# A memory-attention and mixture-of-experts kernel on one core: the half tile's outputs copied before their low parts, W2's split moved to GpSimd in the first layer, W1 loaded in four transfers

## The chip, the cores and the metric

The kernel runs on 1 core of one Trainium2 chip. The metric is the device time of one execution in microseconds (us). Before the change the median of 3 runs is 473.84 us (473.26 to 475.56).

## What is computed

Attention over 32 memory slots in each of 8 batches and 8 heads, and then a layer of 8 experts (one per token) over the 4608 tokens of width 512:

```
a     = softmax(phi)                       # over 32 slots, per token and head
k_m   = einsum('bhsm,bhsd->bhmd', a, k);   v_m = einsum('bhsm,bhsd->bhmd', a, v)
x     = softmax(q @ k_m.T / 8) @ v_m       # heads side by side: (4608, 512)
e     = argmax(normalized(x) @ normalized(expert_emb).T / tau)   # and its softmax weight
out   = weight * (relu(x @ w1[e]) @ w2[e]) # w1: 512 x 1024, w2: 1024 x 512
```

## The kernel before

**One expert per batch.** Work goes batch by batch (b = 0 to 7, 576 tokens each). The kernel counts which expert most tokens of a batch chose (`choose`, L146), loads that expert's W1 and W2, and runs all tokens of the batch through it. Tokens with another expert are done after the last batch by a loop (`rest`) that runs only where there are any.

**Low parts.** A matmul in full fp32 takes several passes. The large products are therefore made of three passes over rounded operands: high by high, high by low, low by high. A tensor's high part is a copy to fp32r, its low part the difference. So attention weights have `aT` (high and low), the projected W1 `gh` and `gl`, the hidden layer `hh` and `hl`, and W2 `wh` and `wl`.

**A batch has three stages on TensorE.**
- `project` (L531) multiplies the batch's values with W1: four PSUM tiles `pg`. ScalarE rounds each to gh, VectorE subtracts for gl.
- `first` (L546) makes the hidden layer: 16 groups of six matmuls, eight (f = 0 to 7) for each half of the tokens (s = 0, 1), each into a PSUM tile `ph` of 128 x 288. ScalarE applies Relu into hh (L560), VectorE makes hl from the same PSUM tile and hh (L561), and in the second half ScalarE copies the last 64 tokens in plain fp32 as `h4`, called h in the trace (L565).
- `second` (L568) makes the output in five tiles. The first is the half tile: the last 64 tokens, 32 plain fp32 matmuls of h4 by w2s (L579). Then four tiles of 128 tokens follow, each of 8 groups of three matmuls (L590). ScalarE scales each result by the tokens' weight into `ys`, and GpSimd issues the store.

The PSUM tiles pg, ph, py and some of po share four buffers (`mm`), so a group of the first layer can begin only when the tile four before it has been read.

**W2's split.** `split_w` (L524) rounds one of W2's eight row blocks into wh (with `scalar.copy` unless another copy is given) and has GpSimd subtract for wl (L528). `must` in `batch` (L670) makes sure that a block is split, in the order of the program, before the first tile uses it.

**The order is written by hand.** Every engine works through its own queue in the program's order. `steps` (L607) makes two lists of places: `first[0..15]`, one after each group of the first layer, and `second[0..39]`, one after each group of the second (0 to 7 the half tile, 8 to 15 the first tile, and so on). While batch b goes through its layers, these places hold the attention of batch b+1 and the softmax of batch b+2:
- `fill`, `weigh` and `divide` are VectorE's work on the scores of b+1, one half g at a time: transpose (L63), maximum (L70), subtract it (L72), ScalarE's Exp (L74), then sum (L81), a small add (L82), reciprocal (L83), product (L84), and `turn` transposes the result into `aw` (L90, L92).
- `attend` (L94) multiplies aw with the values on TensorE (`po`, L101), and `norm` follows on VectorE.
- `choose` counts the experts, and SyncE loads W1 (`load_w1`, L358) and W2 (`load_w2`, L364), `parts` splits aw (GpSimd subtracts, L518), and `keep` stores aw and the values to DRAM.
- `late` (L211) is the row of small VectorE operations on 128 x 5 and 128 x 40 elements that make the tokens' weights (L179 to L208), with one Exp on ScalarE (L198) in between. Batch 0 does its own in `first`, between the groups; the other batches have theirs in the second layer of the batch before.

SyncE's DMAs take eight semaphores in turn, and each waits for the one issued eight before it.

Of the kernel before, what the change touches and what calls it, by code (L numbers as in the profile page):

```python
# [12 lines left out]
AF = mybir.ActivationFunctionType  # L13
# [8 lines left out]
N, DM, E, FF = B * S, H * D, 8, 1024  # L22
NG = 2
NC = 4
# [4 lines left out]
HS = S // 2  # L29
# [187 lines left out]
class Kernel:  # L217
# [139 lines left out]

    def load_w1(self, e, halves=False):  # L358

        for k in range(2):  # L360
            c, f = (slice(NC), slice(512 * k, 512 * k + 512)) if halves else (slice(2 * k, 2 * k + 2), slice(FF))
            self.nc.sync.dma_start(self.w1s[:, c, f], self.w1[bass.ds(e, 1), :, c, f].rearrange("a p c f -> (a p) c f"))

    def load_w2(self, e):  # L364
# [181 lines left out]
    def first(self, n):  # L546

        nc = self.nc
        gh, gl, (ah, al) = self.gh, self.gl, self.aT
        for s in range(2):  # L550
            to = slice(s * HS, s * HS + HS)
            for f in range(8):
                p = self.mm([P, HS], f"ph{n}_{s}{f}")
                fs = slice(f * P, f * P + P)
                for g in range(NG):
                    for k, (w, x) in enumerate(((gh, ah), (gh, al), (gl, ah))):
                        nc.tensor.matmul(  # L557
                            p, lhsT=w[:, g, fs], rhs=x[:, g, to], start=g == 0 and k == 0, stop=g == 1 and k == 2
                        )
                nc.scalar.activation(self.hh[:, f, to], p, AF.Relu)  # L560
                nc.vector.scalar_tensor_tensor(  # L561
                    out=self.hl[:, f, to], in0=p, scalar=0.0, in1=self.hh[:, f, to].bitcast(F32), op0=ALU.max, op1=ALU.subtract
                )
                if s:
                    nc.scalar.activation(self.h4[:, f], p[:, HS - 64 :], AF.Relu)  # L565
                yield

    def second(self, n, gate, put, must):  # L568
# [38 lines left out]
    def steps(self, b, t, u):  # L607


        first, second = ([[] for _ in range(n)] for n in (16, 40))  # L610

        for f in (0, 3, 6) if b else ():
            first[f].append(lambda: self.split_w(self.nc.gpsimd.tensor_copy))
        for f in () if b else (9, 11, 13, 15):
            first[f].append(self.split_w)
        for n in (0, 1, 2, 4, 5) if b else (0, 0, 1, 1):
            second[n].append(self.split_w)
        if not b:
            late = t.late()
            first[1] += [lambda: self.flip(1, 0), lambda: t.attend(4)]  # L620
# [5 lines left out]
        if u:  # L626
            c, o = b + 1, 0 if b else 3
            first[0 + o].append(lambda: self.block(c, 1))
            first[2 + o].append(lambda: self.flip(c, 1))
            first[4 + o].append(lambda: self.scores(c))  # L630

            places = (first[6], first[8], first[10], first[12]), (first[12], first[14], second[0], second[3])
            if not b:
                places = (second[0], second[0], second[0], second[4]), (second[4], second[4], second[4], second[7])
            all = slice(0, BL)
            for g in range(NG):
                work = u.weigh((g,), all)
                places[g][0].append(lambda g=g: u.fill((g,), all, [self.sT[:, i] for i in range(NG)]))
                for at in places[g][1:]:
                    at.append(lambda work=work: next(work, None))  # L640
            for at, g in zip((second[0], second[3]) if b else (second[4], second[7]), range(NG)):
                at.append(lambda g=g: (u.divide((g,), all), u.turn((g,), all)))
            o = 0 if b else 7
            second[14 + o].append(lambda: u.attend(0, 1, pt=self.mm))
            second[15 + o].append(lambda: u.norm(0, 1))
            second[16 + o].append(lambda: u.attend(2, 3))
            second[17 + o].append(lambda: u.norm(2, 3))
            second[18 + o].append(lambda: u.attend(4, pt=self.mm))
            second[20 + o] += [lambda: self.load_w2(u.choose()), lambda: u.norm(4), self.parts, lambda: self.keep(c)]
            second[21 + o] += [u.owner, u.flags]  # L650
            after = u.late()
            for n in (24, 25, 26, 28, 29, 30):
                second[n + o].append(lambda: next(after))
            second[30 + o].append(lambda: list(after))
            m = b + 2
            if m < B:
                for g in range(NG):
                    second[11 + 3 * g + o].append(lambda g=g: self.softmax(m, (g,)))
                second[18 + o].append(lambda: self.shares(m))
                second[22 + o].append(lambda: [self.turn(m, i, min(i + 4, 10)) for i in (0, 4, 8)])  # L660
                second[27 + o] += [lambda: self.slots(m, 0), lambda: self.block(m, 0)]
                second[31 + o].append(lambda: self.flip(m, 0))
        return first, second

    def batch(self, b, t, u):
# [248 lines left out]
```

## Time and profile before

| | |
|---|---|
| median of 3 runs | 473.84 us |
| the profiled execution | 472.12 us, of which the span is 470.2 us |
| TensorE's mean granted clock | 0.979 |
| busy TensorE (PE), its weight loads (PEld) | 428.2 us, 337.7 us |
| busy VectorE (DVE), ScalarE (ACT), GpSimd (POOL) | 287.0 us, 196.5 us, 145.1 us |
| HBM read, written | 66.60 MB, 15.20 MB |
| W1: DMAs of 1024 KB, median to landing | 16, 6.4 us |
| W2: DMAs of 512 KB, median to landing | 32, 10.1 us |

A timeline row gives start, duration (us), engine, line, operation, output<-input, shape and count, and in brackets how long the engine sat idle before it and what ended that. A group row ends with busy us, mean ns of one, and the idle time before them with its releaser. Matmuls overlap, so from start to start they are closer than their durations. In a row of stretches stand the busy time of PE, PEld, DVE, ACT and POOL, then the granted clock (1.00 is full), the DMA share and GB/s. SPq and POOLq are queues that issue DMAs.

### The profile page before, as it was taken

Reading aid. Unit: us, or ns where it says so; the run is one execution under the profiler, and the core shown is the slowest. Engines: PE = TensorE matmul, PEld = TensorE weight load, DVE = VectorE, ACT = ScalarE, POOL = GpSimd, SP = SyncE. Lnnn points to the kernel's source line nnn. Section 1 sums busy time; section 2 is a strip of 40 time slices with the busy share of each in tenths; the row PEclk is TensorE's granted clock in tenths of the full one; section 3 lists DMA queues with packets and bytes.
Section 4 is the critical chain, followed back from the end, with each engine's and each line's share of the span. In section 5 each row is a group of like instructions: output and inputs, shape, how many; then the busy total and the mean of one; then the engine's idle time right before and its main releaser. Section 6 shows DMA issues by size and latency. Waiting matters only on the chain. (4 is left out here: it accounts for less than half of the span.)

```text
span 470.2 us, 9244 instructions
## 1 busy us (share of the span) xinstructions
PE 428.2 (91%) x3516; PEld 337.7 (72%) x3516; DVE 287.0 (61%) x838; ACT 196.5 (42%) x510; POOL 145.1 (31%) x153
## 2 busy tenths in 40 slices
PE   3779989999799998999799997999979998999994
PEld 2548748777687967879487775878768795869683
DVE  5685687658873687536972587636787368646100
ACT  4524553366423553345341663235633354225410
POOL 1020281251523242350630515313332506224500
PEclk9869999999999999999999998999999999999998
DMA  8977801894069801985029910498017600292011
GB/s 303 350 279 237 312 0 58 294 333 191 13 224 337 301 1 33 329 305 208 12 92 379 328 67 12 169 365 314 15 36 278 209 1 1 55 369 98 13 46 48
DMA packets 27584, 82.45 MB, mean 175 GB/s; under 512 B 7080, under 2 KB 7464, under 8 KB 25744
## 3 DMA queue, kind: packets, MB, share of 16 engines
q1 hardware_dynamic: 24736, 73.28, 43.8%
q0 software_dynamic: 2688, 8.26, 4.9%
q8 instruction: 29, 0.48, 0.4%
q10 hardware_dynamic: 112, 0.28, 0.2%
q14 instruction: 19, 0.16, 0.1%
HBM read 66.60 MB, written 15.20 MB: 174 GB/s over the span
## 5 line engine op out<-in xcount | busy, mean ns | idle before, releaser
L528 POOL TENSOR_TENSOR wl<-w2s,wh 128x512 fp32r<-128x512 f32 x64 | 85.3, 1353 | 128.5 <-ACT wh L527 126.8
L590 PE MATMUL py<-wl,hh 128*128 128x512 f32 x256 | 102.6, 401 | 6.0 <-POOL wl L528 5.7
L557 PE MATMUL ph<-aT,gh 128*128 128x288 f32 x512 | 105.3, 300 | 1.0 <-DVE gl L541 0.5
L590 PE MATMUL py<-wh,hh 128*128 128x512 f32 x256 | 105.7, 413 | 0.0
L590 PE MATMUL py<-wh,hl 128*128 128x512 f32 x256 | 100.6, 393 | 0.0
L561 DVE SCALAR_TENSOR_TENSOR hl<-ph,hh 128x288 fp32r<-128x288 f32 x128 | 56.7, 455 | 49.0 <-ACT hh L560 48.8
L557 PEld LDWEIGHTS ph<-aT,gh 128*128 128x128 f32 x512 | 81.4, 188 | 5.8 <-DVE gl L541 2.6
L557 PE MATMUL ph<-aT,gl 128*128 128x288 f32 x256 | 75.3, 294 | 0.0
L590 PEld LDWEIGHTS py<-wl,hh 128*128 128x128 f32 x256 | 48.5, 189 | 21.5 <-POOL wl L528 13.2
L560 ACT ACTIVATE hh<-ph 128x288 fp32r<-128x288 f32 x128 | 51.0, 411 | 21.6 <-PE ph L557 21.6
L590 PEld LDWEIGHTS py<-wh,hh 128*128 128x128 f32 x256 | 48.4, 189 | 12.7 <-issue 3.9
L590 PEld LDWEIGHTS py<-wh,hl 128*128 128x128 f32 x256 | 48.4, 189 | 10.1
L698 POOL DMA_DIRECT2D out_dram<-ys x28 | 15.5, 553 | 110.7 <-ACT ys L603 71.3
L541 DVE TENSOR_TENSOR gl<-pg,gh 128x512 fp32r<-128x512 f32 x32 | 20.0, 685 | 48.0 <-ACT gh L540 48.0
L557 PEld LDWEIGHTS ph<-aT,gl 128*128 128x128 f32 x256 | 48.0, 188 | 0.0
L603 ACT ACTIVATE ys<-py,gate 128x512 f32<-128x512 f32 (+1 forms) x39 | 25.0, 641 | 55.1 <-issue 29.4
L518 POOL TENSOR_TENSOR aT<-aw,aT 128x576 fp32r<-128x576 f32 (+2 forms) x18 | 23.3, 1310 | 61.3 <-DVE aT L517 61.3
L101 PE MATMUL po<-vv,aw 128*128 128x136 f32 x160 | 26.0, 298 | 11.7 <-DVE aw L90 11.7
L101 PEld LDWEIGHTS po<-vv,aw 128*128 128x128 f32 x160 | 23.7, 201 | 16.0 <-DVE aw L90 13.4
L579 PE MATMUL py<-w2s,h 128*64 128x256 f32 x256 | 31.3, 386 | 4.0 <-ACT h L565 4.0
L565 ACT ACTIVATE h<-ph 128x64 f32<-128x64 f32 x64 | 14.3, 224 | 34.3 <-DVE hl L561 34.3
L579 PEld LDWEIGHTS py<-w2s,h 128*64 128x64 f32 x256 | 16.3, 136 | 16.6 <-ACT h L565 10.7
(140 smaller groups left out, 545.0 us busy)
## 6 DMA issues: line engine op xcount, KB each, us to landing
kx<-kv SPq DMA_DIRECT2D x32, 512.0 KB, 6.6
w1s<-w SPq DMA_DIRECT2D x16, 1024.0 KB, 6.4
w2s<-w SPq DMA_DIRECT2D x32, 512.0 KB, 10.1
qt<-qT SPq DMA_DIRECT2D x14, 576.0 KB, 6.5
out_dram<-ys POOLq DMA_DIRECT2D x28, 256.0 KB, 5.8
ex<-phiT SPq DMA_DIRECT2D x16, 288.0 KB, 10.8
ad<-aw SPq DMA_DIRECT2D x8, 576.0 KB, 13.7
kl<-kvt SPq DMA_DIRECT2D x7, 256.0 KB, 3.7
```

Source lines behind the costliest of these rows:

```text
L101: nc.tensor.matmul(po[:, 144 * g : 144 * g + P + E], lhsT=k.aw[:, g, to], rhs=k.vv[:, g], start=True, stop=True)
L518: self.nc.gpsimd.tensor_tensor(out=al, in0=a, in1=ah.bitcast(F32), op=ALU.subtract)
L528: self.nc.gpsimd.tensor_tensor(out=l, in0=x, in1=h.bitcast(F32), op=ALU.subtract)
L541: nc.vector.tensor_tensor(out=self.gl[:, g, f], in0=ps[g], in1=self.gh[:, g, f].bitcast(F32), op=ALU.subtract)
L557: nc.tensor.matmul(p, lhsT=w[:, g, fs], rhs=x[:, g, to], start=g == 0 and k == 0, stop=g == 1 and k == 2)
L560: nc.scalar.activation(self.hh[:, f, to], p, AF.Relu)
L561: nc.vector.scalar_tensor_tensor(out=self.hl[:, f, to], in0=p, scalar=0.0, in1=self.hh[:, f, to].bitcast(F32), op0=ALU.max, op1=ALU.subtract)
L565: nc.scalar.activation(self.h4[:, f], p[:, HS - 64 :], AF.Relu)
L579: nc.tensor.matmul(p[64 * j : 64 * j + 64], lhsT=self.h4[:, f], rhs=self.w2s[:, f, d * j : d * j + d], start=f == 0, stop=f == 7,)
L590: nc.tensor.matmul(p, lhsT=h[:, f, to], rhs=w[:, f], start=f == 0 and k == 0, stop=f == 7 and k == 2)
L603: nc.scalar.activation(y[:, :d], p, AF.Copy, scale=gate[:, i : i + 1])
L698: eng.dma_start(self.out[r : r + P], y)
```

## The change

There are four edits.
- W1 comes in four DMAs of 512 KB where it came in two of 1 MB: for batch 0 by halves of the columns and pairs of row blocks, else by row block.
- In the second half of the first layer, h4's Relu on ScalarE now stands directly behind hh's, ahead of VectorE's hl.
- W2's split: in batches 1 to 7, all eight blocks are rounded and subtracted on GpSimd at `first[0]` to `first[7]`, where three were and five were rounded on ScalarE in the second layer. In batch 0 two blocks each stand at `first[8]`, `[10]`, `[12]` and `[14]`, one rounded on ScalarE and one on GpSimd; they were all rounded on ScalarE, four at `first[9]` to `[15]` and four in the second layer.
- The attends, `choose` with the loads of W1 and W2, `parts`, `keep`, `owner`, `flags` and the turn of the next softmax stand one place later in the second layer; the first attend so comes behind the first tile's last group and no longer ahead of it.

```
     def load_w1(self, e, halves=False):
-        for k in range(2):
-            c, f = (slice(NC), slice(512 * k, 512 * k + 512)) if halves else (slice(2 * k, 2 * k + 2), slice(FF))
+        for k in range(4):
+            i, j = divmod(k, 2)
+            c, f = (slice(2 * j, 2 * j + 2), slice(512 * i, 512 * i + 512)) if halves else (slice(k, k + 1), slice(FF))
...
                 nc.scalar.activation(self.hh[:, f, to], p, AF.Relu)
+                if s:
+                    nc.scalar.activation(self.h4[:, f], p[:, HS - 64 :], AF.Relu)
                 nc.vector.scalar_tensor_tensor(
                     out=self.hl[:, f, to], in0=p, scalar=0.0, in1=self.hh[:, f, to].bitcast(F32), op0=ALU.max, op1=ALU.subtract
                 )
-                if s:
-                    nc.scalar.activation(self.h4[:, f], p[:, HS - 64 :], AF.Relu)
...
-        for f in (0, 3, 6) if b else ():
-            first[f].append(lambda: self.split_w(self.nc.gpsimd.tensor_copy))
-        for f in () if b else (9, 11, 13, 15):
-            first[f].append(self.split_w)
-        for n in (0, 1, 2, 4, 5) if b else (0, 0, 1, 1):
-            second[n].append(self.split_w)
+        for j in range(8):
+            copy = self.nc.gpsimd.tensor_copy if b or j % 2 else None
+            first[j if b else 8 + j // 2 * 2].append(lambda copy=copy: self.split_w(copy))
...
-            second[14 + o].append(lambda: u.attend(0, 1, pt=self.mm))
+            second[15 + o].append(lambda: u.attend(0, 1, pt=self.mm))
...
-            second[20 + o] += [lambda: self.load_w2(u.choose()), lambda: u.norm(4), self.parts, lambda: self.keep(c)]
-            second[21 + o] += [u.owner, u.flags]
+            second[21 + o] += [lambda: self.load_w2(u.choose()), lambda: u.norm(4), self.parts, lambda: self.keep(c)]
+            second[22 + o] += [u.owner, u.flags]
```

ScalarE's queue in the second half of batch 1's first layer before the change (hh is L560, h_97 is h4, L565; in brackets the engines whose work each waits for):

```order
L560 ACTIVATE hh<-ph_10_1302 128x288 [waits PE_49]
L565 ACTIVATE h_97<-ph_10_1302 128x64 [waits DVE_49]
L560 ACTIVATE hh<-ph_11_1314 128x288 [waits PE_49]
L565 ACTIVATE h_97<-ph_11_1314 128x64 [waits DVE_49]
L560 ACTIVATE hh<-ph_12_1324 128x288 [waits PE_49]
L565 ACTIVATE h_97<-ph_12_1324 128x64 [waits DVE_49]
```

The same place in the changed kernel, whose lines are one or two off (hh L561, h4 L563):

```order
L561 ACTIVATE hh<-ph_10_1316 128x288 [waits PE_49]
L563 ACTIVATE h_97<-ph_10_1316 128x64
L561 ACTIVATE hh<-ph_11_1328 128x288 [waits PE_49]
L563 ACTIVATE h_97<-ph_11_1328 128x64
L561 ACTIVATE hh<-ph_12_1338 128x288 [waits PE_49]
L563 ACTIVATE h_97<-ph_12_1338 128x64
```

The copy of h4 stands at the same place in ScalarE's queue but no longer waits for VectorE.

GpSimd's queue from the end of batch 0 (its last store) to batch 1's half tile before the change (L527 rounds W2, L528 subtracts, L705 is the half tile's store):

```order
L698 DMA out_dram<-ys_3_1115 128x512 [waits Activation_49]
L527 CAST wh<-w2s 128x512 [waits DMAHW7_49,PE_49,Pool_49]
L528 TENSOR_TENSOR wl<-w2s,wh 128x512 [waits Pool_49]
L527 CAST wh<-w2s 128x512 [waits PE_49]
L528 TENSOR_TENSOR wl<-w2s,wh 128x512 [waits Pool_49]
L527 CAST wh<-w2s 128x512 [waits DMAHW0_49,PE_49]
L528 TENSOR_TENSOR wl<-w2s,wh 128x512 [waits Pool_49]
L528 TENSOR_TENSOR wl<-w2s,wh 128x512 [waits PE_49,Activation_49]
L528 TENSOR_TENSOR wl<-w2s,wh 128x512 [waits DMAHW1_49,PE_49,Activation_49]
L528 TENSOR_TENSOR wl<-w2s,wh 128x512 [waits PE_49,Activation_49]
L528 TENSOR_TENSOR wl<-w2s,wh 128x512 [waits DMAHW2_49,PE_49,Activation_49]
L528 TENSOR_TENSOR wl<-w2s,wh 128x512 [waits PE_49,Activation_49]
```

And in the changed kernel (L528 rounds, L529 subtracts):

```order
L696 DMA out_dram<-ys_3_1119 128x512 [waits Activation_49]
L528 CAST wh<-w2s 128x512 [waits DMAHW3_49,PE_49]
L529 TENSOR_TENSOR wl<-w2s,wh 128x512 [waits Pool_49]
L528 CAST wh<-w2s 128x512 [waits PE_49]
L529 TENSOR_TENSOR wl<-w2s,wh 128x512 [waits Pool_49]
L528 CAST wh<-w2s 128x512 [waits DMAHW4_49,PE_49]
L529 TENSOR_TENSOR wl<-w2s,wh 128x512 [waits Pool_49]
L528 CAST wh<-w2s 128x512 [waits PE_49]
L529 TENSOR_TENSOR wl<-w2s,wh 128x512 [waits Pool_49]
L528 CAST wh<-w2s 128x512 [waits DMAHW5_49,PE_49]
L529 TENSOR_TENSOR wl<-w2s,wh 128x512 [waits Pool_49]
L528 CAST wh<-w2s 128x512 [waits PE_49]
```

The five roundings that ScalarE had (the subtractions that wait for Activation) now stand on GpSimd, each ahead of its subtraction, and none waits for ScalarE.

GpSimd's queue in batch 0's first and second layer before the change:

```order
L528 TENSOR_TENSOR wl<-w2s,wh 128x512 [waits DMAHW0_49,Activation_49]
L528 TENSOR_TENSOR wl<-w2s,wh 128x512 [waits Activation_49]
L528 TENSOR_TENSOR wl<-w2s,wh 128x512 [waits DMAHW1_49,Activation_49]
L528 TENSOR_TENSOR wl<-w2s,wh 128x512 [waits Activation_49]
L528 TENSOR_TENSOR wl<-w2s,wh 128x512 [waits DMAHW2_49,Activation_49]
L528 TENSOR_TENSOR wl<-w2s,wh 128x512 [waits Activation_49]
L528 TENSOR_TENSOR wl<-w2s,wh 128x512 [waits DMAHW3_49,Activation_49]
L528 TENSOR_TENSOR wl<-w2s,wh 128x512 [waits Activation_49]
```

And in the changed kernel:

```order
L529 TENSOR_TENSOR wl<-w2s,wh 128x512 [waits DMAHW2_49,Activation_49]
L528 CAST wh<-w2s 128x512
L529 TENSOR_TENSOR wl<-w2s,wh 128x512 [waits Pool_49]
L529 TENSOR_TENSOR wl<-w2s,wh 128x512 [waits DMAHW3_49,Activation_49]
L528 CAST wh<-w2s 128x512
L529 TENSOR_TENSOR wl<-w2s,wh 128x512 [waits Pool_49]
L529 TENSOR_TENSOR wl<-w2s,wh 128x512 [waits DMAHW4_49,Activation_49]
L528 CAST wh<-w2s 128x512
L529 TENSOR_TENSOR wl<-w2s,wh 128x512 [waits Pool_49]
L529 TENSOR_TENSOR wl<-w2s,wh 128x512 [waits DMAHW5_49,Activation_49]
L528 CAST wh<-w2s 128x512
L529 TENSOR_TENSOR wl<-w2s,wh 128x512 [waits Pool_49]
```

Four roundings came to GpSimd between the subtractions, which wait for ScalarE in every other block only. VectorE's queue keeps its order through the first layer of both batches and through the two chains of divisions.

More of the change, by code (lines that the diff above doesn't have):

```diff
@@ L643, in steps @@
             o = 0 if b else 7
-            second[14 + o].append(lambda: u.attend(0, 1, pt=self.mm))
[L645 to L648, printed above, removed]
-            second[20 + o] += [lambda: self.load_w2(u.choose()), lambda: u.norm(4), self.parts, lambda: self.keep(c)]
-            second[21 + o] += [u.owner, u.flags]
+            second[15 + o].append(lambda: u.attend(0, 1, pt=self.mm))
+            second[16 + o].append(lambda: u.norm(0, 1))
+            second[17 + o].append(lambda: u.attend(2, 3))
+            second[18 + o].append(lambda: u.norm(2, 3))
+            second[19 + o].append(lambda: u.attend(4, pt=self.mm))
+            second[21 + o] += [lambda: self.load_w2(u.choose()), lambda: u.norm(4), self.parts, lambda: self.keep(c)]
+            second[22 + o] += [u.owner, u.flags]
             after = u.late()
@@ L659, in steps @@
                 second[18 + o].append(lambda: self.shares(m))
-                second[22 + o].append(lambda: [self.turn(m, i, min(i + 4, 10)) for i in (0, 4, 8)])
+                second[23 + o].append(lambda: [self.turn(m, i, min(i + 4, 10)) for i in (0, 4, 8)])
                 second[27 + o] += [lambda: self.slots(m, 0), lambda: self.block(m, 0)]
```

## The prediction, made before the changed kernel ran

> **What bounds the kernel now.** I read the page first, then TensorE's own waits, then its timeline through one batch, then the other engines in the same microseconds.
>
> ```profile
> span 470.2 us, 9244 instructions
> PE 428.2 (91%) x3516; PEld 337.7 (72%) x3516; DVE 287.0 (61%) x838; ACT 196.5 (42%) x510; POOL 145.1 (31%) x153
> ```
>
> TensorE is busy for 91% and no other engine comes near, so the time is TensorE's work plus TensorE's waits. The view of its waits lists those (total, times, longest):
>
> ```profile
> PE po L101 <- DVE aw L90: 11.7, 7, 2.1
> PE py L590 <- POOL wl L528: 5.7, 16, 0.8
> PE py L579 <- ACT h L565: 4.0, 9, 0.6
> PE pg L538 <- DMA w1s<-w: 1.9, 1, 1.9
> ```
>
> One batch (the second, b=1) shows where they lie. TensorE's timeline (start, duration, idle before it):
>
> ```profile
> 111.85 3.26 PE L579 MATMUL py<-w2s,h 128*64 128x256 f32 x28
> 115.50 0.65 PE L579 MATMUL py<-w2s,h 128*64 128x256 f32 x4 [0.40 <-ACT h L565]
> ...
> 120.40 0.50 PE L590 MATMUL py<-wl,hh 128*128 128x512 f32 x1 [0.35 <-POOL wl L528]
> 120.74 0.39 PE L590 MATMUL py<-wh,hl 128*128 128x512 f32 x1
> 120.97 0.40 PE L590 MATMUL py<-wh,hh 128*128 128x512 f32 x1
> 121.64 0.50 PE L590 MATMUL py<-wl,hh 128*128 128x512 f32 x1 [0.28 <-POOL wl L528]
> ...
> 122.21 0.39 PE L101 MATMUL po<-vv,aw 128*128 128x136 f32 x2
> 124.38 0.96 PE L101 MATMUL po<-vv,aw 128*128 128x136 f32 x6 [1.77 <-DVE aw L90]
> ```
>
> Four waits in eleven microseconds, each batch anew: for the half tile's copy (h), twice for a low part of W2 (wl), once for the turned weights (aw). A listed wait is less than it costs, because matmuls overlap: undisturbed they follow each other by 0.23 us (120.74 to 120.97), but 120.97 to 121.64 is 0.67 and the one after a wait follows by 0.34 (120.40 to 120.74). So 0.28 listed costs 0.55, and I add 0.27 to each wait. The half tile agrees: 27 steps in 3.26 less 0.38 make 0.107 each, so matmul 29 was due at 114.84 and began 0.66 late, for 0.40 listed.
>
> **The change, part by part.** *The copy h ahead of hl.* Before, h (ScalarE) waits for hl (VectorE), which reads the same PSUM tile:
>
> ```profile
> L565 ACT ACTIVATE h<-ph 128x64 f32<-128x64 f32 x64 | 14.3, 224 | 34.3 <-DVE hl L561 34.3
> ```
>
> 34.3 us over 64 is 0.54 us in which ScalarE's queue stands, eight times a batch; behind it stand the next hh and W2's casts. Now h follows hh at once and hl waits 0.22 us longer. The last h is then ready some 2 us before the half tile wants it, so its wait goes: 0.67 in each of b=1 to 6, 4.0 us. hl has cover: the first tile reads it only after the half tile's 3.4 us.
>
> *The split of W2.* GpSimd in b=1, and its group of subtractions:
>
> ```profile
> 95.12 0.62 POOL L527 CAST wh<-w2s 128x512 fp32r<-128x512 f32 x1
> 116.03 6.79 POOL L528 TENSOR_TENSOR wl<-w2s,wh 128x512 fp32r<-128x512 f32 x5 [15.06 <-ACT wh L527]
> L528 POOL TENSOR_TENSOR wl<-w2s,wh 128x512 fp32r<-128x512 f32 x64 | 85.3, 1353 | 128.5 <-ACT wh L527 126.8
> ```
>
> Five subtractions in 6.79 us are the pace that the first tile waits for. After it, eight casts and eight subtractions run from 95.1 on: 8 x (0.62 + 1.35) = 15.8 us, done by 111; the first is wanted after the half tile, at 115.3. Cover 4 us; even if W2 lands 2 us later nothing waits. The two wl waits go: (0.62 + 0.55) x 6 = 7.0 us, and two of about 0.55 in the last batch: 8.1 us.
>
> *What GpSimd does to VectorE.* The same chain (sum, small add, reciprocal, product, turn) in b=1 with GpSimd busy, and in b=0 after it had finished:
>
> ```profile
> 120.12 0.71 DVE L81 TENSOR_REDUCE z<-x 128x18 f32<-128x576 f32 x1
> ...
> 121.96 1.48 DVE L84 TENSOR_TENSOR x<-x,z 128x576 f32<-128x576 f32 x1
> ...
> 124.25 0.20 DVE L92 STREAM_TRANSPOSE aw<-x 128x64 f32<-128x64 f32 x1
> ```
>
> ```profile
> 71.08 0.71 DVE L81 TENSOR_REDUCE z<-x 128x18 f32<-128x576 f32 x1
> ...
> 72.34 0.76 DVE L84 TENSOR_TENSOR x<-x,z 128x576 f32<-128x576 f32 x1
> ...
> 73.90 0.20 DVE L92 STREAM_TRANSPOSE aw<-x 128x64 f32<-128x64 f32 x1
> ```
>
> 4.33 us against 3.02: 1.31 less for each of the two chains, so aw is ready at 121.8 in place of 124.45, and about 1.6 earlier again (an estimate: hl is no longer paced by ScalarE's queue), 120.2. TensorE, without its waits (1.84 us), and with the attends one group of three matmuls (0.69) later, asks at 122.21 - 1.84 + 0.69 = 121.1. Margin 0.9 us: the aw wait goes, (1.77 + 0.27) x 6 and 0.35 in the one longer, 12.5 us. The moved steps bring nothing else: `choose` asks for W1 one group later.
>
> Against it: in b=1 to 6 the splits now lie beside hl and one subtraction of a maximum in the first layer.
>
> ```profile
> 98.11 0.46 DVE L561 SCALAR_TENSOR_TENSOR hl<-ph,hh 128x288 fp32r<-128x288 f32 x1 [0.43 <-ACT hh L560]
> 109.28 0.75 DVE L72 TENSOR_TENSOR x<-x,mx 128x576 f32<-128x576 f32 x1
> ```
>
> 98.11 lies inside GpSimd's three splits from 95.12 on (5.7 us) and takes the usual 0.46: hl is not held up. L72 will take about 1.5 as L84 does; that 0.75 is in the 120.2.
>
> *The first batch.* Here VectorE's small gate operations stand between the hl, and GpSimd, which waited for ScalarE's casts there before, now works through from about 52 to 65 (eight subtractions, four casts, 13.3 us). What that does to small operations:
>
> ```profile
> 83.43 2.86 POOL L518 TENSOR_TENSOR aT<-aw,aT 128x576 fp32r<-128x576 f32 x2 [4.47 <-DVE aT L517]
> 84.08 0.85 DVE L179 TENSOR_SCALAR ss<-ss 128x5 f32<-128x5 f32 x1
> 84.96 1.36 DVE L38 TENSOR_SCALAR nrg<-ss 128x5 int32<-128x5 int32 x1
> 56.14 1.28 POOL L528 TENSOR_TENSOR wl<-w2s,wh 128x512 fp32r<-128x512 f32 x1 [1.34 <-ACT wh L527]
> 56.91 0.57 DVE L202 TENSOR_TENSOR eq<-oh,rev 128x40 f32<-128x40 bf16 x1
> 51.76 0.17 DVE L43 SCALAR_TENSOR_TENSOR nrr<-nrr,ss 128x5 f32<-128x5 f32 x1
> ```
>
> L179 and L38 end just as one and the other GpSimd instruction does (84.9, 86.3), L202 with the one at 57.4; a free one takes 0.17. So each small operation with two SBUF inputs, or of L179's kind, waits out GpSimd's current instruction. Five stand ahead of the third hl of the half (L43 and L44 twice, L182); at some 0.7 each that hl comes 3.5 us later, near 57, and TensorE, which needs its PSUM buffer two groups on, pauses about as long. L195 to L197 then hold ScalarE through L198, and the hl whose buffer the half tile needs comes near 60. The first tile starts at 60 + 3.4, and 24 matmuls of 0.23 on, with no wl wait, the second near 69.0. Before they stood at:
>
> ```profile
> 62.28 0.50 PE L590 MATMUL py<-wh,hh 128*128 128x512 f32 x1
> 70.16 0.39 PE L590 MATMUL py<-wh,hh 128*128 128x512 f32 x1
> ```
>
> A gain of 1.1, less a clock drop (below): 0 for this batch. With no holding all its waits would go: what the other batches leave of the h and wl rows, 1.6 and 1.4 in three each, plus 6 x 0.27, about 5. With all eleven small operations held a whole 1.35, 15 us on VectorE, I lose some 3. I take 0 between -3 and +5: the three held rows are the nearest.
>
> The Trainium skill ("SBUF — State Buffer", Who interferes with whom) states this as an exclusive lock: a VectorE instruction with two SBUF inputs and a GpSimd instruction that reads SBUF fully block each other, and the order of issue decides. By that rule every small operation would be held and the first batch would be at its end of -3, the sum 23.6 us. The trace bears out the holding (L179, L38, L202) but not that it is full both ways: five subtractions with two L84 among them took 6.79 us, where 5 x 1.28 + 2 x 0.76 would be 7.9.
>
> *The clock.* The batch with the longest aw wait is followed by this stretch (PEclk third from the end):
>
> ```profile
> 290.00:295.00 5.00, 5.00 (x25) 4.47 (x25) 2.50 (x13) 2.84 (x6) 0.56 (x1) 0.67 0.07 27
> ```
>
> 5 x 0.33 = 1.65 us lost, which goes if the wait goes. The same price is what the 4 us pause in b=0 may cost.
>
> *W1 in four.* At the start the first 512 KB feed the first head group, so about half of the 1.09 us of projection moves into the 1.9 us wait: 0.3, between 0 and 0.5. Later W1 must land before the projection:
>
> ```profile
> 83.35 0.88 SPq L362 DMA_DIRECT2D w1s<-w  x2
> DMA to landing us min/median/max: 5.0/6.4/8.4
> 93.44 1.96 PE L538 MATMUL pg<-w1s,vT 64*32 64x512 f32 x32
> ```
>
> Issue 0.44 each: the second lands by 83.8 + 8.4 = 92.2, 1.2 early, in b=0, the tightest case. Asked 0.7 later, it keeps 0.5; the two more issues delay W2 and the copies to DRAM behind them on SyncE by 0.9, and those have 4 us and more. Cost 0, at worst 1 us once. The Trainium skill ("SBUF — State Buffer", Summary: rules for kernel authors) says one DMA, not several; its fit of 2 us + bytes/436 GB/s, if transfers ran one after another, would add 4 us per load, 3 us once here, and the sum would be 23.6. The issues of 0.44 us overlap in the trace, so I keep 0.
>
> **The sum.** h 4.0 + wl 8.1 + aw 12.5 + clock 1.65 + W1 0.3 + b=0 0 = 26.6 us. The profiled execution took 472.12 (span 470.2 and 1.9 around it), 1.7 under the median 473.84. 472.12 - 26.6 = 445.5; on the median 447.2. I take 447.
>
> **The rivals.** *A: the first batch isn't held up.* The small operations find the gaps between GpSimd's instructions. For it: in b=1 L84 gets in between two subtractions. Against: L179 and L38, held one after the other. Gain 26.6 + 5: 442.
>
> *B: aw still comes late.* The margin is 0.9 us of an estimate; if W2 lands late, GpSimd reaches into the two chains again (+1.3 each). Then TensorE waits up to the old 2 us six times and keeps the clock drop: 447 + 10 = 457; half of it 452. Against: 4 us of cover on GpSimd.
>
> *C: slower; GpSimd in the first layer holds up hl, which frees TensorE's PSUM buffers.* VectorE's work there, in two stretches (third pair of numbers):
>
> ```profile
> 95.00:101.00 6.00, 5.93 (x80) 5.12 (x73) 4.16 (x8) 3.65 (x11) 5.73 (x7) 1.00 1.04 375
> 101.00:112.00 11.00, 11.00 (x121) 10.02 (x121) 7.18 (x16) 6.38 (x22) 0.00 (x0) 1.00 0.95 317
> ```
>
> 24 instructions, 11.3 us. If each waited out a GpSimd instruction, 16 would be through when GpSimd ends at 111, and the other 8 would take until 116: the layer ends 4.4 us later, which is the gain of a batch (24.6 over six, 4.1). With a pause like that the clock drops each time: 447 + 6 x (4.4 + 1.65) = 483. It decides from 4.4 us a batch on. The row at 98.11 speaks against it.
>
> *D: W2 isn't early.* W2 lands only when the half tile begins, the splits start late and the wl waits stay, as does half the aw wait: 447 + 8 + 6 = 461. Against: the cast at 95.12 found W2 there.
>
> **How the numbers follow.** The forecast 0.62 (444 to 451, the ends of b=0), A 0.16, B 0.13, D 0.04, C 0.05 (0.02 of it where stall and gain cancel). 8 in 10 takes the forecast, most of A and half of B: 441 to 456. About 0.5% (2.4 us) is what a measurement here tells from no change; all but C are faster by more: faster 0.95, same 0.02, slower 0.03.
>
> **What would show it.** In the changed profile: no h and wl rows in TensorE's waits after b=0; L84 0.76 in b=1 to 6; GpSimd's last subtraction before the half tile; in b=0 L43, L44 and L182 of 0.6 to 1.3 and a TensorE wait of several us for hl. It is wrong if L101 still waits for aw, or if hl takes longer than 0.46.

## The result, and the profile after

The changed kernel took 446.5 us (median of 4 executions, 445.13 to 450.67) against 473.55 for the kernel before on the same chip (4 executions, 471.49 to 475.56): a ratio of 0.9444, 95% interval 0.9364 to 0.9523. The profiled execution was the longest of the four, 450.67 with a span of 448.5. The first lines of its page:

```profile
span 448.5 us, 9263 instructions
PE 422.5 (94%) x3516; PEld 340.8 (76%) x3516; DVE 272.8 (61%) x838; ACT 174.5 (39%) x471; POOL 167.2 (37%) x192
```

GpSimd (POOL) has 22 us more work, ScalarE (ACT) 22 us less, and TensorE (PE) is nearer to its own work alone. Of the view of TensorE's waits (total, times, longest) these are the rows for hl, W1 and aw:

```profile
PE ph L558 <- DVE hl L564: 3.1, 2, 2.3
PE pg L539 <- DMA w1s<-w: 2.7, 2, 2.3
...
PE po L101 <- DVE aw L90: 1.2, 1, 1.2
```

The rows for h and for wl are gone, and the one wait left for aw lies in the head of the program (23 us), none in b=1 to 6. The first row is new: two waits for hl, both in b=0. Batch b=1 on TensorE, to be laid beside the one in the prediction:

```profile
116.29 3.67 PE L580 MATMUL py<-w2s,h 128*64 128x256 f32 x32
119.89 0.50 PE L591 MATMUL py<-wh,hh 128*128 128x512 f32 x1
...
125.49 1.09 PE L101 MATMUL po<-vv,aw 128*128 128x136 f32 x8
```

The 32 steps of the half tile run in one piece, the 24 matmuls of the first tile follow each other by 0.23 us, and the attend begins without a wait. What made room for it is on the two other engines of that batch. These are GpSimd's first rounding and last subtraction, then the end of VectorE's second chain:

```profile
99.90 0.61 POOL L528 CAST wh<-w2s 128x512 fp32r<-128x512 f32 x1 [0.82 <-PE pg L539]
...
114.63 1.29 POOL L529 TENSOR_TENSOR wl<-w2s,wh 128x512 fp32r<-128x512 f32 x1
```

```profile
122.44 0.76 DVE L84 TENSOR_TENSOR x<-x,z 128x576 f32<-128x576 f32 x1
...
124.01 0.20 DVE L92 STREAM_TRANSPOSE aw<-x 128x64 f32<-128x64 f32 x1
```

The splits take 16.0 us and end 4 us before the first tile's first use. L84 takes 0.76, and aw is there at 124.2, 7.9 us after the half tile's start, where it was 12.6 before (124.45 less 111.85); the attend asks at 125.49, so the margin is 1.3 us.

The two spans are cut here at the same places: the last matmul of key (L141), the first of the first layer, the projections (pg) of b=1 and of b=7, and the end. First the kernel before (its projection of b=1, at 93.44, stands in the prediction), then the changed one:

```profile
24.93 0.19 PE L141 MATMUL key<-oh,ones 128*128 128x8 bf16 x2 [0.67 <-DVE oh L109]
37.68 0.53 PE L557 MATMUL ph<-aT,gh 128*128 128x288 f32 x2
421.02 1.96 PE L538 MATMUL pg<-w1s,vT 64*32 64x512 f32 x32
```

```profile
26.04 0.20 PE L141 MATMUL key<-oh,ones 128*128 128x8 bf16 x2 [0.67 <-DVE oh L109]
40.70 0.54 PE L558 MATMUL ph<-aT,gh 128*128 128x288 f32 x2
97.40 2.45 PE L539 MATMUL pg<-w1s,vT 64*32 64x512 f32 x32
148.78 2.24 PE L539 MATMUL pg<-w1s,vT 64*32 64x512 f32 x32
400.40 1.96 PE L539 MATMUL pg<-w1s,vT 64*32 64x512 f32 x32
```

| stretch | before | changed | gain |
|---|---|---|---|
| start to the last key | 24.93 | 26.04 | -1.1 |
| key to the first layer (W1 arrives) | 12.75 | 14.66 | -1.9 |
| first layer of b=0 to the projection of b=1 | 55.76 | 56.70 | -0.9 |
| six batches, projection to projection | 327.6 | 303.0 | 24.6 |
| b=7 and the end | 49.2 | 48.1 | 1.1 |
| span | 470.2 | 448.5 | 21.7 |

All of the gain lies in the six batches and the last one. Ahead of them this execution lost 3.9 us, and the experiments had to say how much of that belongs to the change.

### The profile page after: what moved, and what is told of

Same layout as the page of the kernel before. It is cut to its first block, busy times and chain, and to the rows that moved or that the text cites. A ratio compares the mean times of both kernels' runs of the same rounds, so it can differ in the third digit from the quotient of the medians.

```text
span 448.5 us, 9263 instructions
## 1 busy us (share of the span) xinstructions
PE 422.5 (94%) x3516; PEld 340.8 (76%) x3516; DVE 272.8 (61%) x838; ACT 174.5 (39%) x471; POOL 167.2 (37%) x192
## 5 line engine op out<-in xcount | busy, mean ns | idle before, releaser
L558 PE MATMUL ph<-aT,gh 128*128 128x288 f32 x512 | 106.4, 302 | 3.6 <-DVE hl L564 3.1
L591 PE MATMUL py<-wl,hh 128*128 128x512 f32 x256 | 99.8, 390 | 0.0
L529 POOL TENSOR_TENSOR wl<-w2s,wh 128x512 fp32r<-128x512 f32 x64 | 84.9, 1328 | 26.6 <-ACT wh L528 21.7
L558 PEld LDWEIGHTS ph<-aT,gh 128*128 128x128 f32 x512 | 82.4, 190 | 8.0 <-DVE hl L564 3.5
L564 DVE SCALAR_TENSOR_TENSOR hl<-ph,hh 128x288 fp32r<-128x288 f32 x128 | 55.7, 449 | 33.8 <-ACT hh L561 27.0
L561 ACT ACTIVATE hh<-ph 128x288 fp32r<-128x288 f32 x128 | 51.5, 415 | 33.0 <-PE ph L558 32.5
L591 PEld LDWEIGHTS py<-wh,hh 128*128 128x128 f32 x256 | 48.1, 188 | 12.5 <-issue 3.9
L528 POOL CAST wh<-w2s 128x512 fp32r<-128x512 f32 x60 | 37.4, 623 | 0.8 <-PE pg L539 0.8
L580 PEld LDWEIGHTS py<-w2s,h 128*64 128x64 f32 x256 | 18.2, 142 | 10.2 <-issue 1.9
L101 PE MATMUL po<-vv,aw 128*128 128x136 f32 x160 | 24.4, 295 | 1.2 <-DVE aw L90 1.2
```

What stands on the lines that cost most here:

```text
L101: nc.tensor.matmul(po[:, 144 * g : 144 * g + P + E], lhsT=k.aw[:, g, to], rhs=k.vv[:, g], start=True, stop=True)
L528: (copy or self.nc.scalar.copy)(h, x)
L529: self.nc.gpsimd.tensor_tensor(out=l, in0=x, in1=h.bitcast(F32), op=ALU.subtract)
L558: nc.tensor.matmul(p, lhsT=w[:, g, fs], rhs=x[:, g, to], start=g == 0 and k == 0, stop=g == 1 and k == 2)
L564: nc.vector.scalar_tensor_tensor(out=self.hl[:, f, to], in0=p, scalar=0.0, in1=self.hh[:, f, to].bitcast(F32), op0=ALU.max, op1=ALU.subtract)
L580: nc.tensor.matmul(p[64 * j : 64 * j + 64], lhsT=self.h4[:, f], rhs=self.w2s[:, f, d * j : d * j + d], start=f == 0, stop=f == 7,)
```

## The experiments

The theory was the forecast's: in b=1 to 6 the batch is set by TensorE's last wait, aw; in b=0 GpSimd holds VectorE's small gate operations. Against it stood that each edit brings its own term and no more, and that b=0's stall and the late start come from somewhere else. Each experiment's medians are of 4 or 5 executions, beside the kernel before on the same chip. "The stretch of b=0" is the third row of the table, "a batch" is from projection to projection; 54.75 and 50.9 are the batch of the kernel before and of the changed one in the main (before, b=4 took 56.67; the stretch of b=6 is some 3 us shorter in every kernel).

**The copy h alone.** The kernel before with this edit only:

```
                 nc.scalar.activation(self.hh[:, f, to], p, AF.Relu)
+                if s:
+                    nc.scalar.activation(self.h4[:, f], p[:, HS - 64 :], AF.Relu)
                 nc.vector.scalar_tensor_tensor(
...
-                if s:
-                    nc.scalar.activation(self.h4[:, f], p[:, HS - 64 :], AF.Relu)
```

> The kernel before with one edit: the half tile's copy h ahead of hl. The forecast gave this edit 4.0 us by itself (0.67 in each of b=1 to 6), with the rest of what it does (hl about 1.6 us earlier) counted under aw. Theory: the terms overlap. In b=1 to 6 the attend's aw ends the last wait of the batch, so a batch shortens by what aw comes earlier, which is the hl part alone: aw was ready 12.6 us after the half tile's start before (124.45 against 111.85) and 7.9 in the changed kernel (124.2 against 116.29), 4.7 earlier, of which 2.6 are the two chains no longer held by GpSimd; 2.1 are left for h. So the waits for h go, the waits for aw stay near 1.8 listed, and the batch takes 52.7 us in place of 54.75: some 12.6 us over six batches, about 460. Rival (each edit brings its own term): 4.0 us, batches of 54.1, about 469. Second rival (the wait only moves to wl, aw is unmoved): 473 to 474.

Measured: 456.89 us against 472.32, ratio 0.9655 (0.9621 to 0.9689), and batches of 52.8. TensorE, VectorE and GpSimd in b=1 of this kernel (its half tile starts at 110.02):

```profile
120.61 0.96 PE L101 MATMUL po<-vv,aw 128*128 128x136 f32 x6 [1.68 <-DVE aw L90]
```

```profile
111.29 1.84 DVE L72 TENSOR_TENSOR x<-x,mx 128x576 f32<-128x576 f32 x1
...
114.64 1.50 DVE L84 TENSOR_TENSOR x<-x,z 128x576 f32<-128x576 f32 x1
...
118.92 0.76 DVE L84 TENSOR_TENSOR x<-x,z 128x576 f32<-128x576 f32 x1
```

```profile
111.24 7.31 POOL L528 TENSOR_TENSOR wl<-w2s,wh 128x512 fp32r<-128x512 f32 x5 [12.09 <-ACT wh L527]
```

The waits for h went, and those for wl with them: the roundings stand behind h in ScalarE's queue, and the five subtractions begin 1.2 us after the half tile's start, where it was 4.2 before (116.03 less 111.85). The wait for aw is as long as ever, because TensorE comes earlier by what it no longer waits for. A batch is shorter by 1.95 us, what aw comes earlier (2.1 expected). VectorE's second chain begins 2 us earlier, but it is held as much as before, at other operations: the five subtractions, now earlier too, lie beside its L72 (1.84 us in place of 0.75), while its last L84 is free. The rival's 4.0 us was not even a third of the gain. Of the 15.4 us, 11.9 are the six batches, 1.9 the stretch of b=0 (53.9), 1.3 the last batch; the expected 460 counted the six batches alone and was 3 us too long.

**The split alone**, in b=1 to 7:

```
-        for f in (0, 3, 6) if b else ():
-            first[f].append(lambda: self.split_w(self.nc.gpsimd.tensor_copy))
+        for j in range(8 if b else 0):
+            first[j].append(lambda: self.split_w(self.nc.gpsimd.tensor_copy))
...
-        for n in (0, 1, 2, 4, 5) if b else (0, 0, 1, 1):
+        for n in () if b else (0, 0, 1, 1):
```

> The kernel before with one edit: W2 rounded and split on GpSimd alone in the first layer of b=1 to 7 (b=0, the order of h and hl, the attends and W1 as before). Theory (terms overlap, aw ends the last wait): the two waits for wl go, L84 takes 0.76 in place of 1.48 and aw comes 2.6 us earlier, the waits for h stay (0.40 listed), and a wait for aw of about 0.3 listed is left: batches of 52.1 us in place of 54.75, with 1.1 in the last batch and the clock drop of 1.65 some 18 us, about 455. Rival (the terms add): wl 8.1 and aw's 2.6 in six batches, 15.7, with the clock 25 us, about 448. Second rival (GpSimd does not hold VectorE's chain): L84 stays at 1.48, the wl gain is taken back at aw, batches of 54.7, 1 to 2 us, about 472.

Measured: 453.2 us against 472.32, ratio 0.9577 (0.9539 to 0.9614), batches of 52.06. TensorE and VectorE in b=1:

```profile
115.65 0.65 PE L579 MATMUL py<-w2s,h 128*64 128x256 f32 x4 [0.40 <-ACT h L565]
121.85 0.96 PE L101 MATMUL po<-vv,aw 128*128 128x136 f32 x6 [0.33 <-DVE aw L90]
```

```profile
117.21 0.76 DVE L84 TENSOR_TENSOR x<-x,z 128x576 f32<-128x576 f32 x1
...
120.15 0.76 DVE L84 TENSOR_TENSOR x<-x,z 128x576 f32<-128x576 f32 x1
```

The batch is as expected to the tenth: the half tile waits for h as before, the waits for wl are gone, both L84 take 0.76, and 0.33 of waiting for aw is left. The total is 1.8 us below the expected 455. So GpSimd did hold the chains.

**The attends alone**, the last of the four edits (`second[14 + o]` and the rows behind it one higher) in the kernel before:

> The kernel before with one edit: the attends and the steps behind them one group of three matmuls later. Theory (aw's time is set by VectorE and GpSimd, not by TensorE's place in its queue): aw is ready as before, TensorE does 0.69 us of other work first, the waits for aw fall from 1.77 to about 1.1 listed: batches of 54.1 in place of 54.75, 4.1 us over six, and 1.65 more if the shorter wait no longer brings the clock down: 468 to 469.5. Rival: the steps behind the attends (norm, load, late) become later and something else waits for them, nothing gained: 473.5.

Measured: 466.07 us against 472.32, ratio 0.9849 (0.9814 to 0.9884), batches of 54.07. The row of b=1:

```profile
124.44 0.96 PE L101 MATMUL po<-vv,aw 128*128 128x136 f32 x6 [0.54 <-DVE aw L90]
```

aw comes at the same time (the attend goes on at 124.44, before at 124.38), and TensorE did three more matmuls first, so that the wait fell by 1.2 listed: the group's 0.69, and a third wait for wl that now falls into it. The gain is 6.3 us: 4.1 for six groups, about 1.6 for the clock drop of b=4, which is gone.

**The attends back**: the changed kernel without that edit.

> The changed kernel with the attends and the steps behind them one group earlier again, as before the change. The forecast had the waits for aw go by the earlier aw (no longer held by GpSimd, hl not paced by ScalarE) with 0.9 us of margin, of which the move gave 0.69. In the changed kernel aw was ready at 124.2 in b=1 and the attend began at 125.49: 1.3 us of margin, 0.6 left without the move. So no wait for aw in b=1 to 6 and the time is the same, 446.5 within 1. Rival (the move carries part of the gain): a wait for aw in each of the six batches, at most 0.69 longer each, and up to 450.6.

Measured: 445.61 us against 472.76, ratio 0.9426 (0.9402 to 0.9451); no wait for aw in b=1 to 6, batches of 50.9. Here the move brings nothing. Alone it was worth 6.3.

**h back**: the changed kernel with h behind hl again.

> The changed kernel with h behind hl again, all else as changed. Theory (ScalarE's queue stands for 0.5 us behind each hl and paces hl): the waits for h come back in b=1 to 6 (0.67 each) and hl and with it aw are about 2.1 us later than in the changed kernel, where the margin was 1.3: TensorE, 0.67 later itself, waits for aw a little (0.1 to 0.3 listed), together about 0.9 to 1.2 a batch: batches of 51.9, 6 us over six, about 452. Rival (with five roundings gone from ScalarE, its queue has time and h is early in either order): 50.9 a batch, no change, 446.

Measured: 451.16 us against 472.32, ratio 0.9538 (0.9503 to 0.9573), batches of 51.5 in the main:

```profile
116.57 0.65 PE L580 MATMUL py<-w2s,h 128*64 128x256 f32 x4 [0.40 <-ACT h L566]
```

The wait for h came back and costs its 0.6; a wait for aw did not come, against the 0.1 to 0.3 expected. The second chain's L72 begins 3.24 us after the half tile's start, as late as in the kernel before (3.26), where it is 1.27 in the changed kernel. So h behind hl paces VectorE whether ScalarE has the roundings or not, and the rival fails. The 2.0 us that aw loses are just covered by the margin of 1.3 and the 0.65 that TensorE itself comes later. The time is 4.7 us above the changed kernel's, 3.4 of it in the six batches; the two intervals overlap.

The three edits alone gain 15.4, 19.1 and 6.3 us, 40.8 in all; together, W1's four transfers and b=0's new splits among them, they gain 27.

**W1 in two.** The changed kernel with `load_w1` as before:

```
-        for k in range(4):
-            i, j = divmod(k, 2)
-            c, f = (slice(2 * j, 2 * j + 2), slice(512 * i, 512 * i + 512)) if halves else (slice(k, k + 1), slice(FF))
+        for k in range(2):
+            c, f = (slice(NC), slice(512 * k, 512 * k + 512)) if halves else (slice(2 * k, 2 * k + 2), slice(FF))
```

> The changed kernel with W1 in two transfers again (as before the change), all else changed. The forecast gave the four transfers 0.3 us of gain, once, at the start, and nothing later: undone, the time is 446.8 (446.5 + 0.3), and from the last matmul of key (L141) to the first matmul of the first layer it takes no less than in the changed kernel (14.7 us, 26.04 to 40.70). Rival: the four transfers cost time at the start, since the same stretch took 12.8 us in the kernel before (24.93 to 37.68): undone, the stretch is 12.8 again, and the time 444.6. Both expect no other change: 50.9 us from batch to batch, b=0 stalled for hl as in the changed kernel.

Measured: 444.82 us against 472.76, ratio 0.9426 (0.9392 to 0.946): by the time alone not to be told from the changed kernel. The stretch from key to the first layer was 12.76, as the rival had it. But it is not one number. Over all profiles of this study it was, with W1 in four, 14.66, 11.44, 14.34, 11.83 and 12.14 (mean 12.9); with W1 in two, 12.75, 12.76, 12.80, 12.62, 12.76, 12.70 and 14.26 (mean 12.95). The best and the worst of the four-way loads on TensorE, the run with the first batch's splits as before and the changed kernel:

```profile
31.21 1.06 PE L539 MATMUL pg<-w1s,vT 64*32 64x512 f32 x8 [1.02 <-DMA w1s<-w]
32.65 1.06 PE L539 MATMUL pg<-w1s,vT 64*32 64x512 f32 x8 [0.38 <-DMA w1s<-w]
```

```profile
34.06 1.06 PE L539 MATMUL pg<-w1s,vT 64*32 64x512 f32 x8 [2.33 <-DMA w1s<-w]
35.49 1.87 PE L539 MATMUL pg<-w1s,vT 64*32 64x512 f32 x8 [0.37 <-DMA w1s<-w]
```

Where the first transfer lands soon, the projection does start early, as the forecast had it (1.02 of waiting in place of 1.85). In the changed kernel's profile the wait is 2.33; the first matmul on the first transfer began 6.4 us after its issue (27.64 to 34.06), against 4.8 in the other run (26.37 to 31.21). The second eight matmuls then take 1.87 in place of 1.06, at the lower clock (0.66 over the 5 us from 34 on, 1.00 in the other run from 31.2 on). Why it landed later, no run shows. The third of the four issues on SyncE took 3.3 us there in place of 0.4:

```profile
28.84 3.32 SPq L363 DMA_DIRECT2D w1s<-w  x1
```

But it stands behind the two that these waits belong to, and the best run has one of 1.7 as well (four of the five profiles with W1 in four have one of 1.7 to 3.3, those with W1 in two none over 0.65). No gain or loss on the mean can be shown at the start. Later there is a small loss: with W1 in two, every projection after b=0 took 1.96; in four, that of b=1 or b=2 or both took 2.24 to 2.48 in each of the five profiles (2.45 and 2.24 in the rows above), 0.3 to 0.8 us in all.

**The first batch's splits as before the change**, the rest changed:

```
-        for j in range(8):
-            copy = self.nc.gpsimd.tensor_copy if b or j % 2 else None
-            first[j if b else 8 + j // 2 * 2].append(lambda copy=copy: self.split_w(copy))
+        for j in range(8 if b else 0):
+            first[j].append(lambda: self.split_w(self.nc.gpsimd.tensor_copy))
+        for f in () if b else (9, 11, 13, 15):
+            first[f].append(self.split_w)
+        for n in () if b else (0, 0, 1, 1):
+            second[n].append(self.split_w)
```

> The changed kernel with the split of W2 in the first batch as before the change (roundings on ScalarE, four pairs in the first layer, four in the second); b=1 and later as changed. Theory (GpSimd's instructions hold the small gate operations of VectorE that stand ahead of hl): the waits for hl (0.82 and 2.26 us listed) and the clock drop behind them go, L43, L44 and L182 take 0.17 to 0.2 again, but the two to four waits for wl come back (2.2 us listed before); from the first matmul of the first layer to the projection of b=1 it takes about 52.7 us (56.7 in the changed kernel, 55.8 in the one before, whose h waits of 3.1 are gone), so the time is about 442.5. Rival (the stall comes from the new order of h and hl, or from the gate chain itself): the waits for hl stay, 56.7 us or more, 446.5.

Measured: 442.63 us against 472.76, ratio 0.9373 (0.9342 to 0.9405), the stretch of b=0 53.3. The total is as expected, the way not quite. First the changed kernel, VectorE and GpSimd in its first batch:

```profile
54.90 1.28 DVE L43 SCALAR_TENSOR_TENSOR nrr<-nrr,ss 128x5 f32<-128x5 f32 x1
56.21 0.52 DVE L44 SCALAR_TENSOR_TENSOR nrg<-nrg,nrr 128x5 f32<-128x5 f32 x1
...
58.12 1.19 DVE L44 SCALAR_TENSOR_TENSOR n<-nrg,nrr 128x5 f32<-128x5 f32 x1
59.34 0.52 DVE L182 TENSOR_SCALAR n<-n 128x5 f32<-128x5 f32 x1
```

```profile
54.86 1.30 POOL L529 TENSOR_TENSOR wl<-w2s,wh 128x512 fp32r<-128x512 f32 x1 [20.10 <-ACT wh L528]
56.10 0.60 POOL L528 CAST wh<-w2s 128x512 fp32r<-128x512 f32 x1
56.79 2.49 POOL L529 TENSOR_TENSOR wl<-w2s,wh 128x512 fp32r<-128x512 f32 x2
59.22 0.61 POOL L528 CAST wh<-w2s 128x512 fp32r<-128x512 f32 x1
```

Each of VectorE's ends with one of GpSimd's: 56.18 with 56.16, 56.73 with 56.70, 59.31 with 59.28, 59.86 with 59.83. In the experiment three of the five operations run free (0.17), but two subtractions (50.80 to 53.48) still meet the others:

```profile
51.29 0.82 DVE L43 SCALAR_TENSOR_TENSOR nrr<-nrr,ss 128x5 f32<-128x5 f32 x1
...
52.35 1.16 DVE L182 TENSOR_SCALAR n<-n 128x5 f32<-128x5 f32 x1
```

One wait for hl of 1.47 is left, where 0 was expected, with the clock at 1.00; no wait for wl came back, and one of 0.65 for aw did. The reason is h again: ScalarE, no longer standing behind hl, rounds earlier, and GpSimd starts 14.6 us after the first matmul of the first layer, where it was 15.8 in the kernel before. The run with h alone, whose splits are those of the kernel before, has the like wait for hl (1.46).

**The gates earlier.** The changed kernel with its splits where they are, and the gate operations of b=0 ahead of them:

```
-            for f in (5, 6, 8, 9, 11, 12):
+            for f in (4, 5, 5, 6, 6, 7):
                 first[f].append(lambda: next(late))
```

> The changed kernel with the first batch's gate operations three to five groups earlier, ahead of the split of W2; the splits where the change put them. Theory (holding by GpSimd): L43, L44, L182 and L195 run while GpSimd is idle and take 0.17 to 0.2, hl no longer comes late, the waits for hl (3.1 us listed) and the clock drop go; GpSimd's splits run as before to about 68 us, now later than TensorE wants the last of them, so 1 to 2 us of wl wait come: the stretch from the first matmul of the first layer to the projection of b=1 takes 52 to 53 us in place of 56.7, the time is about 442.5. Rival (GpSimd holds hl itself, or the stall is the first batch's number of VectorE operations): hl waits of 2 us and more stay, 446.5.

Measured: 444.52 us against 472.76, ratio 0.9393 (0.9358 to 0.9427), the stretch of b=0 53.8. The small operations run in 0.17, and TensorE's waits in b=0 are:

```profile
51.75 0.54 PE L558 MATMUL ph<-aT,gh 128*128 128x288 f32 x2 [0.43 <-DVE hl L564]
53.26 0.51 PE L558 MATMUL ph<-aT,gh 128*128 128x288 f32 x2 [0.44 <-ACT h L563]
68.04 0.50 PE L591 MATMUL py<-wl,hh 128*128 128x512 f32 x1 [1.24 <-POOL wl L529]
```

The stall of 3.1 us went with the holding, the clock drop with the stall, and the wl wait came, as expected. The stretch missed the expected 52 to 53 by 0.8 and the time the expected 442.5 by 2. New are the first two rows: the exponential of the gates (L198) stands on ScalarE until VectorE's long chain gives it its input.

**Both, with W1 in two.** Gates from the third group on (3, 4, 4, 5, 6, 6); the splits of b=0 in the groups 7 to 14 in one kernel, as before the change in the other.

> The changed kernel with W1 in two transfers, the first batch's gate operations from the third group on (3, 4, 4, 5, 6, 6) and its eight splits in the groups 7 to 14, roundings on ScalarE and GpSimd in turn. Theory (the first batch's stall is small operations held behind GpSimd; what was left with the gates early, 53.8 us, was ScalarE standing for the exponential, 0.43 and 0.44 listed, and the last wl 1.24): none of the three is left, from the first matmul of the first layer to the projection of b=1 it takes 51 to 52 us (55.5 with W1 in two and nothing else), the start 12.8, batches of 50.9: 441 us. Rival (the splits now start while gate operations are still to come, or the first batch has another bound near 53.5 us): 53 to 54 us there and 443 in all.

> The changed kernel with W1 in two transfers, the first batch's gate operations from the third group on, and its splits as before the change (four pairs in the first layer, four in the second, roundings on ScalarE). Theory: with the splits as before it took 53.3 us from the first matmul of the first layer to the projection of b=1, of which the wait for hl (1.47) came from L43 and L182 held behind GpSimd and the one for aw (0.65) from the chain beside the late splits; the first goes, the second may stay: 51 to 51.7 us, 440.5 to 441.5. Rival (GpSimd, free earlier, is still behind TensorE in the second layer): waits for wl come back, 53 us and more, 443.

Measured: 440.55 us against 473.26, ratio 0.9312 (0.9286 to 0.9339), the stretch of b=0 51.9; and 441.28, ratio 0.9326 (0.9307 to 0.9345), 51.45. The only wait of TensorE over 0.2 in the first one's first batch:

```profile
53.73 0.53 PE L557 MATMUL ph<-aT,gh 128*128 128x288 f32 x2 [0.36 <-DVE hl L563]
```

Both come out as the theory had it, the one at 440.55 for 441, the other at 441.28 for 440.5 to 441.5. They cannot be told from each other; the intervals of both lie below that of the changed kernel, so they are faster than both kernels, by 5 to 6 us against the changed one.

## Why the prediction was right

**The six batches** were to give h 4.0, wl 7.0, aw 12.5 and clock 1.65, that is 25.15 us; they gave 24.6, with 0.8 lost to W1's two later projections. The last batch was to give 1.1 and gave 1.1.

**The terms were right only as a sum.** "Copy h: 4.0" is neither what that edit brings alone (15.4) nor what its removal costs (451.16, 4.7 us above the changed kernel). What made the sum hold was the step that asked when TensorE would want aw once its other waits were gone, and when aw would be there: 121.1 against 120.2, a margin of 0.9; measured 1.3. The same step shows where it is loose: it counted 0.69 of that margin as the attends' move, and without the move nothing changes, since the remaining 0.6 is enough.

**aw earlier by 4.2** (1.31 twice and 1.6): 4.7 measured. The rows of five profiles tell the two causes apart in b=1 (us; the chain is VectorE's second, from L72 to the end of the last L92):

| kernel | half tile's start to the chain | the chain | sum: aw is ready |
|---|---|---|---|
| before | 3.26 | 9.34 | 12.60 |
| h alone | 1.27 | 9.39 | 10.66 |
| split alone | 3.26 | 6.65 | 9.91 |
| h back | 3.24 | 6.66 | 9.90 |
| changed | 1.27 | 6.65 | 7.92 |

The order of h and hl sets when the chain begins (2.0 us, estimated at 1.6), and GpSimd's splits set how long it takes (2.7 us, estimated at 2.62); neither touches the other's share. This is the mechanism of the forecast.

**GpSimd's cover of 4 us**: its last subtraction ended at 115.9, and the first tile began at 119.9.

**L72 would be held to 1.5**: not so. In b=1 it came first, and GpSimd was the one that waited, its rounding taking 1.16 for 0.61:

```profile
113.33 0.75 DVE L72 TENSOR_TENSOR x<-x,mx 128x576 f32<-128x576 f32 x1
```

```profile
113.39 1.16 POOL L528 CAST wh<-w2s 128x512 fp32r<-128x512 f32 x1
```

In b=2 to 6 the rounding came first, and L72 took 0.95 to 0.98, held for some 0.2 us. So the holding goes both ways and whoever starts first keeps the other out, which is what the Trainium skill says ("SBUF — State Buffer", Who interferes with whom). The prediction doubted that rule by a sum with two L84 among five subtractions. That reading was wrong: the second L84 (121.96 to 123.44) ended after the fifth subtraction (122.82), so only one lay among them, and it did cost GpSimd its 0.5 us, in the longest of the five (minimum, median, maximum in ns, kernel before):

```profile
L528 POOL TENSOR_TENSOR wl<-w2s,wh x5: 1268/1287/1799, 116.0 to 121.6; 128x512 fp32r<-128x512 f32 x5
```

**The first batch: 0, between -3 and +5.** -0.9 in this execution, by the mechanism named: L43, L44 and L182 of 0.52 to 1.28, then waits for hl of 0.82 and 2.26, and the clock:

```profile
55.00:60.00 5.00, 2.39 (x16) 1.92 (x15) 4.83 (x9) 1.56 (x7) 4.84 (x6) 0.95 1.05 406
60.00:65.00 5.00, 4.53 (x20) 3.69 (x22) 4.11 (x14) 2.93 (x11) 3.29 (x4) 0.50 0.12 47
65.00:70.00 5.00, 5.00 (x34) 3.23 (x31) 4.86 (x9) 1.05 (x2) 4.68 (x5) 0.87 0.00 0
```

5 x (0.05 + 0.50 + 0.13) = 3.4 us at the lower clock, twice the 1.65 that the prediction put beside its 1.1 of gain. But that is this one execution. The profiles of the attends back and of W1 in two have the same stall in b=0, and there it cost 1.7 us of clock, here with W1 in two:

```profile
56.50:61.50 5.00, 5.00 (x28) 4.05 (x30) 4.11 (x14) 2.93 (x11) 3.29 (x4) 0.66 0.05 16
```

Their stretches of b=0 took 55.80 and 55.52, no loss and 0.2 of gain against the 55.76 before, which is the forecast's 0. Why the clock stayed low longer in the one execution, no run shows. Rival A would have needed the small operations free; the two last experiments give it by another order (51.9 and 51.45), 3.9 and 4.3 us under the 55.76 before, where the prediction had about 5.

**W1: +0.3 at the start, 0 later.** The gain is not shown: single executions gain 1.3 or lose 1.9 in that stretch, and the mean is the same with two transfers. The 0 was 0.3 to 0.8 us of loss, inside the 1 us that the prediction allowed.

**The rivals.** B: no wait for aw came. D: W2 was there at 99.9, when the first splits began. C: hl is not held by GpSimd anywhere; over all its 128 instructions (minimum, median, maximum in ns) it took

```profile
L564 DVE SCALAR_TENSOR_TENSOR hl<-ph,hh x128: 411/456/459, 42.6 to 416.5; 128x288 fp32r<-128x288 f32 x128
```

and TensorE's only waits for hl are those of b=0, behind the small operations.

**The two totals.** The median 446.5 met 447; the profiled execution was to take 445.5 and took 450.67, of which 1.1 stood ahead of anything the change touches (the last key comes at 23.7 to 26.3 over all profiles), 2.2 are W1's start against the forecast's 0.3, 0.9 the first batch and 0.8 the two later projections. That the median came within 0.5 us is luck in part: the changed kernel's four executions lie between 445.13 and 450.67, which is wider than the terms of W1 and of b=0.

## What to carry to other kernels

Where several waits stand in a row in each round of a loop, ask for each edit how much earlier the last one of them ends, with all the earlier waits gone; the parts' gains overlap (40.8 alone, 27 together), and an edit worth 6 us alone can be worth nothing beside the others. An engine that is given more work can still make its neighbour faster, if it does the work at another time: moving GpSimd's splits off VectorE's chain paid more (2.7 us a batch alone) than the waits for the splits themselves (1.17). Small VectorE operations like L43, L44 and L182, which took 0.5 to 1.3 us in place of 0.17 beside GpSimd, are worth moving away from GpSimd's busy stretch where they stand ahead of an operation that frees a buffer.

## What was not expected of the hardware

In the batches, TensorE's clock fell behind each of five single waits of 2.04 to 2.26 us (in the profiles of before, changed, attends back, W1 in two and h alone), and behind none of twelve of 1.46 to 1.78. In the run with h alone four batches that waited 1.68 or 1.69 for aw took 52.8 us; the one that waited 2.04 took 54.75, and its clock (third from the end) was:

```profile
280.00:285.00 5.00, 5.00 (x29) 4.63 (x27) 2.63 (x13) 2.80 (x6) 0.56 (x1) 0.72 0.00 0
```

The Trainium skill ("TensorE: Matmul & The Clock Gate", Part 1) has the clock halved after an idle window of about 3.4 us; here 2.0 was enough. A single wait is not the whole rule: at the start, where the clock had only just come up from 0.50, it fell to 0.66 behind waits for W1 of 1.80 (split alone) and 1.85 (before) too, and stayed at 1.00 behind one of 1.44 (h back). Why the limit lies there, no run showed.
